# Norm pieces issued at once and Wo ahead of PV, for every chunk needed next, in a one-core transformer block

## The chip, the cores and the metric

The kernel runs on one core of a Trainium2 chip. Its engines work from queues of their own: TensorE (PE; its weight loads are shown as PEld), VectorE (DVE), ScalarE (ACT), GpSimd (POOL) and SyncE (SP, which here only issues DMA). They wait for each other by semaphores, and each runs its instructions in the order in which they were issued to it. The metric is the device time of one execution in microseconds, less is better.

## The reference

One transformer block over 2048 tokens of width 1024, batch 1, all in bfloat16: layer norm, attention with 32 query heads of 32 that share one key and one value head, a residual, a second layer norm, a gated feed-forward of width 3584, a residual.

```python
def _A_ref(x, wq, wk, wv, wo):
    q = (x @ wq).reshape(B, S, H, Dh).transpose(0, 2, 1, 3)
    k = x @ wk
    v = x @ wv
    p = softmax(einsum("bhqd,bkd->bhqk", q, k) * Dh ** -0.5)
    o = einsum("bhqk,bkd->bhqd", p, v)
    return o.transpose(0, 2, 1, 3).reshape(B, S, H * Dh) @ wo

def _B_ref(x, w_gate, w_up, w_down):
    return (sigmoid(x @ w_gate) * (x @ w_up)) @ w_down

h = x + _A_ref(layernorm(x), wq, wk, wv, wo)
h2 = h + _B_ref(layernorm(h), w_gate, w_up, w_down)
```

## The kernel before

The tokens are cut into 8 chunks of 256 (`NQC`, `QC`), each of two tiles of 128 tokens (`TPQ`). Keys, values and queries are made first. Then attention for chunk c+1 runs while the feed-forward of chunk c runs between its pieces.

**Attention** goes in 512 bursts (`NB`). A chunk has 8 groups of four heads (a group is one g = 8c + q), and a group has 8 bursts (`BPG`), each over 256 keys. `s_burst(k)` (L637) issues eight matmuls of scores into S_ps; two exponentials on ScalarE (`one_exp`, L660) turn them into P, which lies in a ring of 18 tiles, 9 bursts (`RP`); `ring_need(k)` tells how far PV must have come before burst k has a place in it. For most groups VectorE adds P over pairs of key tiles (`add_pair`: pair L694, merge L703), so that the sums of the softmax cost few matmuls (L734). `pv_group(g)` multiplies P by V (L754) in one bank of X_ps; its evacuation copies and transposes out (L772, L773), then `recip` (L778, L780) and `mult` (L784) write the group's attention output into QT. These two are put into VectorE's waiting list `lo` unless the group is the very last of chunk 0.

**Wo, residual, second norm.** When all 8 groups of a chunk have their output, four `wo_group`s (two token tiles, two halves of the width; eight matmuls of 128x512 each, L316) form the attention result. Their evacuation adds x (L844) and calls `stats2`: `bn_stats` of the half (L866), after the second half `bn_aggr` (L870), then mean, variance plus eps, and two powers on GpSimd (L331, L339, L342, L344), then `norm` on VectorE (L348) and a transposing DMA into QT (`transpose2`, L487; on SyncE's queue, for the last chunk on ScalarE's). Only for chunk 0 are the statistics issued in the evacuation itself, with the eps addition on VectorE (L873), and the norm put at the head of its list (`first`). For other chunks the pieces wait in `lo` under a chain "l0" or "l1", and are issued when `dve_fill` finds room by the planner's clock.

**Feed-forward.** Per chunk 14 gate groups and 14 up groups in turn (`half_group`, 16 matmuls of 128x256 each, L932), tanh on ScalarE (L951), the product on VectorE (L971), then four down groups (28 matmuls of 128x512 each, L996) with the evacuation L1006, which adds the residual and stores. Weights for gate and up come in halves of 512 KB through SyncE's queue into 21 places as these come free (`load_halves`). All of it stands in one list, `ffn_list`; the first gate group of a chunk may be taken only when both tiles' norms are there.

**The planner.** The order on all engines is made while the program is built, by a loop with a clock for each engine (`k_pe`, `k_dve` and others) and costs written in the code. PV, Wo, feed-forward and query groups share two X_ps banks. In each turn the loop takes the first that applies: a burst, if the ring and S_ps have room; the PV group under way; the current group if the next chunk is starved; a Wo group of chunk 0 ahead of all else (`first`); a new PV group; the current or next group of Wo, queries or feed-forward. `force` issues items of `lo` until a condition holds.

Of the kernel before, what the change touches and what calls it, by code (L numbers as in the profile page):

```python
# [84 lines left out]
def bass_sequential_preLN__grouped_kv_mqa__glu_gated_glu__prompt_kernel(  # L85
# [18 lines left out]
    NQ = D // P  # L104
    QC = 256
    NQC = S // QC
    TPQ = QC // P
# [5 lines left out]
    NB = NQC * NQ * BPG  # L113
    WSL = NQ * BPG
    RP = 18
    HR = 5
    NGU = 4
    G_SUM, NPB, NO_SUM = 3, 4, (NQ,)
    HG = 3
    WD_AT, WD_GAP, WD_LATE = 6, 6, 6  # L120
# [5 lines left out]
    with ExitStack() as es:  # L126
# [13 lines left out]
        hact_flat = sb("hact", [NFT * QC])  # L140
        gu = sb("gu", [NGU, 512], F32)
        wgu = sb("wgu", [4, DT, 256])
# [78 lines left out]
        def _(unused):  # L221
# [383 lines left out]
            def ring_need(k):  # L605

                r = ring(k)
                if r is None or r < 2 * BPG + 1:
                    return 0
                return r - 2 * BPG if r <= 2 * BPG + BPG else r - BPG  # L610
# [33 lines left out]
            pv_done = [0]  # L644
# [71 lines left out]
            def pv_group(g):  # L716
                c, q = g // NQ, g % NQ
# [51 lines left out]
                def evac(bank, tick):  # L769
                    force("a", lambda: g < 1 or g - 1 in ols_read)  # L770
                    need(dve, tick, ols_read.get(g - 1))
                    dve.tensor_copy(out=ols[:, 0:QC], in_=bank[:, 0:QC])  # L772
                    free = c_dve.inc(dve.transpose(ols[:, QC:2 * QC], bank[:, QC:2 * QC]), 0.7, 0.08)  # L773
                    t_ = [None]

                    def recip():
                        need(dve, free)
                        r_ = c_dve.inc(dve.reciprocal(l8[:], ols[:, QC:2 * QC].rearrange("p (a b) -> p a b", b=32)[:, :, 0]), 0.23)  # L778
                        need(dve, r_)
                        t_[0] = c_dve.inc(dve.transpose(ols[:, QC:2 * QC], l8[:].unsqueeze(2).to_broadcast([P, QC // 32, 32])), 0.4)  # L780

                    def mult():
                        need(dve, t_[0])
                        ot_val[(c, q)] = ols_read[g] = c_dve.inc(dve.tensor_tensor(  # L784
                            out=QT[:, q, c * QC:(c + 1) * QC], in0=ols[:, 0:QC], in1=ols[:, QC:2 * QC],
                            op=ALU.mult), 0.4)
                    if g == NQ - 1:
                        force("a", lambda: not any(x[0] == "a" for x in lo))
                        recip()
                        mult()  # L790
                    else:
                        put("a", 0.65, recip, lambda: when(free))
                        put("a", 0.4, mult, lambda: when(t_[0]))
                    return free
                return _Group(items, evac, (), "pv")


# [40 lines left out]
            def wo_group(c, tt, dc):  # L838
                t = c * TPQ + tt

                def evac(bank, tick):
                    need(dve, tick, hx_val[t])
                    hv = hx[:, t % HR, dc * 512:(dc + 1) * 512]
                    h_val[t] = c_dve.inc(dve.tensor_tensor(out=hv, in0=bank, in1=hv, op=ALU.add), 0.61, 0.08)  # L844
                    stats2(c, tt, dc)
                    if dc == DC - 1:
                        h_done.add(t)
                    return h_val[t]
                items = mm_list([(QT[:, q, c * QC + tt * P:c * QC + (tt + 1) * P], wo[:, q, dc * 512:(dc + 1) * 512])
                                 for q in range(NQ)], lambda bank: bank, 512)  # L850
                g = _Group(items, evac, [wo_val[0]] + [ot_val[(c, q)] for q in range(NQ)])
                g.first = c == 0
                return g

            ln2_pow = {}

            def stats2(c, tt, dc):
                t, first = c * TPQ + tt, c == 0
                idx = NT + t
                src = hx[:, t % HR, :]  # L860
                chain = "l%d" % (t % 2)
                h_tick = h_val[t]

                def part(cc):
                    need(dve, h_tick)
                    ins = dve.bn_stats(st[:, idx % 4, cc, :], src[:, cc * 512:(cc + 1) * 512])  # L866
                    k_dve[0] += 0.64
                    if cc == DC - 1:
                        need(dve, c_dve.inc(ins))
                        st2_val[t] = c_dve.inc(dve.bn_aggr(mv[:, idx, :], st[:, idx % 4, :, :]), 0.2)  # L870
                        if first:
                            need(dve, st2_val[t])
                            v = c_dve.inc(dve.tensor_scalar(out=vz[:, idx:idx + 1], in0=mv[:, idx:idx + 1, 1], scalar1=EPS_B,  # L873
                                                            scalar2=None, op0=ALU.add), 0.1)
                            ln2_pow[t] = ln_pow(idx, v)
                            ln_mean(idx)
                            ln2_pow[t] = (c_pool, c_pool.n)
                        else:
                            ln2_pow[t] = ln_rstd(idx, st2_val[t])

                def norm():
                    before = hn_read[t - TPQ] if c > 0 else xnT_read[NT - TPQ + tt]
                    hn_val[t] = ln_norm(src, hn[:, tt, :], idx, st2_val[t], ln2_pow[t], before)
                    transpose2(c, tt)
                if first:
                    part(dc)
                else:
                    put(chain, 0.85 if dc else 0.64, lambda: part(dc), lambda: when(h_tick))
                if dc == DC - 1:
                    put(chain, 0.5, norm, lambda: None if t not in ln2_pow or c > 0 and t - TPQ not in hn_read else  # L890
                        when(ln2_pow[t]), first)
# [52 lines left out]
            def gate_group(c, fp):  # L944
                n = c * NFP + fp
                slot = gu[:, n % NGU, :]

# [15 lines left out]
            def up_group(c, fp):  # L963
                n = c * NFP + fp
                slot = gu[:, n % NGU, :]

# [54 lines left out]
            q_list = collections.deque()  # L1021
            wo_list = collections.deque((c, tt, dc) for c in range(NQC) for tt in range(TPQ) for dc in range(DC))
            ffn_list = collections.deque()
# [7 lines left out]
            cur, pv = [None], [None]  # L1031

            def busy(g):
                return g is not None and bool(g.items)

            def wo_ready():
                if not wo_list:
                    return False
                c, tt, dc = wo_list[0]
                t = c * TPQ + tt  # L1040
                return t in hx_val and when(hx_val[t]) <= k_pe[0] and all(
                    (c, q) in ot_val and when(ot_val[(c, q)]) <= k_pe[0] for q in range(NQ))

            def wo_c():
                return wo_list[0][0] if wo_list else -1
# [82 lines left out]
            for p in range(1, BPG):  # L1128
# [11 lines left out]
                q = p + 2  # L1140
# [45 lines left out]
            while True:  # L1186
# [6 lines left out]
                kk = k[0]  # L1193
# [12 lines left out]
                if busy(pv[0]):  # L1206
                    t_ = pv[0].items[0][2]()
                    if t_ > k_pe[0] + (2.5 * T_SW if pe_mode[0] == "pv" else 0.02):
                        if not busy(cur[0]):
                            cur[0] = next_group()  # L1210
                        if busy(cur[0]):
                            run_item(cur[0])
                            continue
                        if t_ > k_pe[0] + 0.6 and can_s:
                            k_pe[0] += 0.05
                            dve_fill(k_pe[0])
                            continue
                    run_item(pv[0])
                    if not pv[0].items and pv_done[0] == NB - BPG and not pr_given[0]:
                        pr_given[0] = True  # L1220
                        for i in range(H_PR, len(halves) - 1):
                            half_free.append((i, [(c_pv, c_pv.n), (c_dve, c_dve.n)]))
                        load_halves()
                    continue
                starved = not q_list and bool(ffn_list) and ffn_list[0][0] == "g" and ffn_list[0][1] * TPQ + 1 not in h_done
                if starved and not busy(cur[0]) and wo_ready():
                    cur[0] = next_group()
                if starved and busy(cur[0]):
                    run_item(cur[0])
                    continue  # L1230
                if not busy(cur[0]) and wo_list and wo_list[0][0] == 0 and wo_ready():
                    cur[0] = next_group()
                if busy(cur[0]) and cur[0].first:
                    run_item(cur[0])
                    continue
                if pv_ready and (pe_mode[0] == "s" or not can_s) and not (busy(cur[0]) and cur[0].left() < 1.0):
# [59 lines left out]
```

## Time and profile before

| | us |
|---|---|
| median of 3 runs | 1132.54 (1132.32 to 1133.71) |
| profiled execution, its time | 1132.68 |
| profiled execution, its span | 1130.9 |
| TensorE busy | 1090.1 |
| ScalarE busy | 1006.6 |
| of it exponentials into the ring, L660 x992 | 931.8, mean 1137 ns with overlap |
| VectorE busy | 860.1 |
| pairs L694 x480 and merges L703 x360 | 324.9 and 248.0 |
| GpSimd busy | 67.4 |
| DMA, mean | 133 GB/s |

The span is what the profiler saw from the first instruction to the last; the execution's own time has 1.8 us more around it. Busy times of one engine add up to less than the span by what it idled. Matmuls overlap in the array, so a busy TensorE is not one at its peak. A window row gives, for a stretch of the span, the busy time of each engine with its instructions in brackets, the granted TensorE clock (1.00 is full), the DMA engines' mean busy share and GB/s. A row of waits gives who waited for whom: total us, times, longest. In the timeline, a bracket after an instruction is the idle time before it and what ended that.

### The profile page before, as it was taken

The page shows a single profiled execution, that of the slowest core. Times are in us where ns is not written, and L with a number is a line of the kernel's source. Part 1 is how long each engine was busy: PE and PEld are TensorE (multiplying, and loading weights), DVE is VectorE, ACT ScalarE, POOL GpSimd, SP SyncE. Part 2 cuts the span into 40 slices and gives each one's busy share as a digit, 9 for nine tenths or more (in the row PEclk, how much of TensorE's full clock was granted, in tenths as well). Part 3 has the DMA queues.
Part 4 walks back from the last instruction along what each step waited for, and adds up shares of the span by engine and source line. Part 5 has one row for each costly group of instructions (what it writes and reads, how often), then busy time and mean ns, then how long its engine had stood idle before and what let it go on. Part 6 is the DMA issues. An engine that isn't in the chain of part 4 may idle for free.

```text
span 1130.9 us, 33101 instructions
## 1 busy us (share of the span) xinstructions
PE 1090.1 (96%) x14332; PEld 660.1 (58%) x14395; DVE 860.1 (76%) x1538; ACT 1006.6 (89%) x1150; POOL 67.4 (6%) x142
## 2 busy tenths in 40 slices
PE   7999999999899999999899999999899989999998
PEld 5663447754476545764477545764377535775784
DVE  7769977778878798788887798878887788884111
ACT  6999999999999999999999999999999999990110
POOL 4410010000100000000000010000100010001000
PEclk9999999999999999999999999999999999999999
DMA  8834117860366415661266514662167522769600
GB/s 196 176 81 171 39 39 220 231 187 24 88 187 191 118 29 150 192 191 47 61 194 195 147 31 134 193 192 57 34 185 213 160 39 62 209 193 263 180 1 19
DMA packets 282065, 150.38 MB, mean 133 GB/s; under 512 B 38592, under 2 KB 276160, under 8 KB 281920
## 3 DMA queue, kind: packets, MB, share of 16 engines
q1 hardware_dynamic: 274144, 137.65, 45.2%
q0 software_dynamic: 2544, 9.44, 2.4%
q8 instruction: 113, 1.85, 0.7%
q10 hardware_dynamic: 5232, 1.18, 0.7%
q14 instruction: 32, 0.26, 0.1%
HBM read 136.18 MB, written 4.19 MB: 124 GB/s over the span
## 4 chain that ended last, share of the span: by engine, by line
PE 71%; ACT 11%; DVE 11%; issue 4%; POOL 2%; DMA 1%; DVEq 0%; ACTq 0%
PE X_ps L932 34%; PE X_ps L996 12%; PE S_ps L637 10%; ACT Pr L660 9%; PE X_ps L754 8%; PE X_ps L316 5%; DVE pairs L694 3%; DVE pairs L703 3%; PE X_ps L734 1%; DVE st L866 1%; ACT hact L660 1%; POOL sd L342 1%; DVE hx L844 1%; POOL rs L344 1%; ACT QT L660 0%
## 5 line engine op out<-in xcount | busy, mean ns | idle before, releaser
L660 ACT ACTIVATE Pr<-S_ps 128x1024 bf16<-128x1024 f32 x992 | 931.8, 1137 | 8.8 <-PE S_ps L637 8.6
L694 DVE TENSOR_TENSOR pairs<-Pr 128x1024 bf16<-128x1024 bf16 x480 | 324.9, 684 | 76.6 <-ACT Pr L660 74.4
L932 PE MATMUL X_ps<-QT,wgu 128*128 128x256 bf16 x2096 | 267.3, 274 | 0.9 <-DVE ols L773 0.7
L703 DVE TENSOR_TENSOR pairs<-pairs 128x1024 bf16<-128x1024 bf16 x360 | 248.0, 689 | 22.3 <-DVE pairs L694 0.5
L932 PEld LDWEIGHTS X_ps<-QT,wgu 128*128 128x128 bf16 x2096 | 191.7, 98 | 58.3 <-issue 34.9
L996 PE MATMUL X_ps<-zone,hact 128*128 128x512 bf16 x849 | 206.6, 380 | 11.4 <-issue 4.9
L637 PE MATMUL S_ps<-QT,kT 32*128 32x256 bf16 x4096 | 204.4, 274 | 13.5 <-ACT Pr L660 7.0
L932 PE MATMUL X_ps<-QT 128*128 128x256 bf16 x1312 | 167.0, 273 | 0.2 <-DVE ols L773 0.2
L637 PEld LDWEIGHTS S_ps<-QT,kT 32*128 32x128 bf16 x4096 | 61.2, 92 | 156.9 <-ACT Pr L660 122.9
L754 PE MATMUL X_ps<-Pr,V 128*32 128x256 bf16 x3968 | 140.7, 275 | 4.0 <-DVE ols L773 1.5
L951 ACT ACTIVATE gu<-X_ps 128x512 f32<-128x512 f32 x112 | 74.4, 665 | 76.9 <-PE X_ps L932 75.9
L996 PEld LDWEIGHTS X_ps<-zone,hact 128*128 128x128 bf16 x896 | 78.4, 97 | 110.1 <-issue 25.2
L932 PEld LDWEIGHTS X_ps<-QT 128*128 128x128 bf16 x1312 | 121.8, 98 | 31.5 <-issue 17.1
L971 DVE SCALAR_TENSOR_TENSOR hact<-gu,X_ps 128x512 bf16<-128x512 f32 x112 | 76.5, 683 | 66.8 <-PE X_ps L932 65.8
L754 PEld LDWEIGHTS X_ps<-Pr,V 128*32 128x32 bf16 x3968 | 98.2, 97 | 30.3 <-issue 17.2
L316 PE MATMUL X_ps<-zone 128*128 128x256 bf16 (+2 forms) x512 | 77.1, 290 | 3.4 <-issue 2.4
L316 PE MATMUL X_ps<-wo,QT 128*128 128x512 bf16 x240 | 59.4, 380 | 1.8 <-issue 1.6
L331 POOL CAST mean<-mv 128x1 f32<-128x1 bf16 x28 | 9.9, 353 | 789.4 <-DVE mv L870 778.5
L316 PEld LDWEIGHTS X_ps<-zone 128*128 128x128 bf16 x512 | 36.7, 97 | 33.2 <-issue 16.7
L1006 DVE SCALAR_TENSOR_TENSOR hx<-X_ps,hx 128x512 bf16<-128x512 f32 x32 | 21.9, 684 | 42.2 <-PE X_ps L996 42.1
L772 DVE COPY ols<-X_ps 128x256 f32<-128x256 f32 x64 | 27.0, 421 | 16.0 <-PE X_ps L734 13.6
L316 PEld LDWEIGHTS X_ps<-wo,QT 128*128 128x128 bf16 x256 | 22.0, 98 | 29.2 <-issue 8.6
(76 smaller groups left out, 473.5 us busy)
## 6 DMA issues: line engine op xcount, KB each, us to landing
wgu<-in_B_w_gate_dram SPq DMA_DIRECT2D x73, 512.0 KB, 4.8
wgu<-in_B_w_up_dram SPq DMA_DIRECT2D x58, 512.0 KB, 4.8
QT<-in_B_w_up_dram SPq DMA_DIRECT2D x49, 512.0 KB, 4.9
QT<-in_B_w_gate_dram SPq DMA_DIRECT2D x33, 512.0 KB, 4.8
zone<-in_B_w_down_dram POOLq DMA_DIRECT2D x14, 512.0 KB, 5.4
hx<-in_A_x_dram SPq DMA_DIRECT2D x16, 256.0 KB, 3.5
out_dram<-hx SPq DMA_DIRECT2D x32, 128.0 KB, 1.7
Pr<-in_B_w_gate_dram SPq DMA_DIRECT2D x5, 512.0 KB, 7.9
```

Source lines behind the costliest of these rows:

```text
L316: ins = pe.matmul(sel(bank), lhsT=a, rhs=b, start=(i == 0), stop=(i == last))
L637: ins = pe.matmul(S_ps[:, bank, kt * QC:(kt + 1) * QC], lhsT=kT4[DH * j:DH * (j + 1), (2 * b + kt) * P:(2 * b + kt + 1) * P], rhs=QT[DH * ...
L660: c_e.inc(act.activation(out=p_tile(k, n % 2), in_=S_ps[:, 2 * pr:2 * pr + 2, :].rearrange("p a (b q) -> p (a b) q", q=QC), func=ACTF.Exp, ...
L694: add_half[k] = slot_use[slot] = c_dve.inc(dve.tensor_tensor(out=pairs[:, slot, :].rearrange("p (j q) -> p j q", j=4), in0=p4[:, :, 0, :], ...
L703: slot_use[x] = slot_use[y] = c_dve.inc(dve.tensor_tensor(out=pairs[:, x, :], in0=pairs[:, x, :], in1=pairs[:, y, :], op=ALU.add), T_ADD, ...
L754: ins = pe.matmul(bank[DH * j:DH * (j + 1), 0:QC], lhsT=V[:, 2 * b + kt, :], rhs=rhs(j), start=first and is_sum, stop=last and not is_sum, ...
L772: dve.tensor_copy(out=ols[:, 0:QC], in_=bank[:, 0:QC])
L932: ins = pe.matmul(bank[:, j * QC:(j + 1) * QC], lhsT=halves[i][:, dt, j * P:(j + 1) * P], rhs=QT[:, dt, c * QC:(c + 1) * QC], start=(dt == ...
L951: tanh_val[n] = c_act.inc(act.activation(out=slot, in_=bank, func=ACTF.Tanh, scale=0.5), T_TANH, 0.1)
L971: hact_val[(c, 2 * fp + 1)] = gu_read[n] = c_dve.inc(dve.scalar_tensor_tensor(out=hact[:, 2 * fp:2 * fp + 2, :], in0=slot.rearrange("p (a ...
L996: ins = pe.matmul(bank, lhsT=hact[:, ft, tt * P:(tt + 1) * P], rhs=wd[:, ft, dc * 512:(dc + 1) * 512], start=(ft == 0), stop=(ft == NFT - 1))
L1006: v = c_dve.inc(dve.scalar_tensor_tensor(out=hv, in0=bank, scalar=0.5, in1=hv, op0=ALU.mult, op1=ALU.add), 0.61, 0.08)
```

## The change

A new function `urgent(c)` tells whether chunk c is needed next: no query groups are left, the list of feed-forward has at most `NEAR` = 1 down group at its head, and what follows is of chunk c. Four places use it:

- in `pv_group`, for a chunk's last group, the waiting reciprocals and products are issued and this group's own at once;
- in `stats2`, the statistics go in with the evacuation, the eps addition on VectorE, and the norm at the head of its list, as for chunk 0 before;
- `wo_group`s get the mark `first`, and the planner takes a ready Wo group as soon as no other group is under way;
- a group marked `first` is run ahead of the next PV group, but, for chunks other than 0, only while the next burst has a place for its P (`can_s0`). `wo_c()` is the chunk of the next Wo group that is left, -1 if none.

```diff
+    NEAR = 1
...
-                    if g == NQ - 1:
+                    if g == NQ - 1 or q == NQ - 1 and urgent(c):
                         force("a", lambda: not any(x[0] == "a" for x in lo))
                         recip()
                         mult()
...
-                g.first = c == 0
+                g.first = c == 0 or urgent(c)
                 return g
...
+            def urgent(c):
+
+                downs = 0
+                while downs < len(ffn_list) and ffn_list[downs][0] == "down":
+                    downs += 1
+                return not q_list and downs <= NEAR and downs < len(ffn_list) and ffn_list[downs][1] == c
+
             def stats2(c, tt, dc):
-                t, first = c * TPQ + tt, c == 0
+                t, first = c * TPQ + tt, c == 0 or urgent(c)
...
+                can_s0 = kk < NB and pv_done[0] >= ring_need(kk)
                 starved = not q_list and bool(ffn_list) and ffn_list[0][0] == "g" and ffn_list[0][1] * TPQ + 1 not in h_done
...
-                if not busy(cur[0]) and wo_list and wo_list[0][0] == 0 and wo_ready():
+                if not busy(cur[0]) and wo_list and (wo_list[0][0] == 0 or urgent(wo_list[0][0])) and wo_ready():
                     cur[0] = next_group()
-                if busy(cur[0]) and cur[0].first:
+                if busy(cur[0]) and cur[0].first and (can_s0 or wo_c() == 0):
                     run_item(cur[0])
                     continue
```

## The prediction

> **What bounds the kernel now.** I began with the page's first part, then took 28 us windows and, inside them, 4 us windows, the list of waits on TensorE, and the timeline around each chunk's turn from attention to feed-forward.
>
> ```profile
> PE 1090.1 (96%) x14332; PEld 660.1 (58%) x14395; DVE 860.1 (76%) x1538; ACT 1006.6 (89%) x1150; POOL 67.4 (6%) x142
> ```
>
> TensorE is busy for 96% and ScalarE for 89%. The kernel runs in two regimes. Up to about 1018 us ScalarE's exponentials set when a burst of scores may come; TensorE fills the time between bursts with PV, Wo and feed-forward. After the last exponential only feed-forward is left and TensorE alone sets the end. So the end moves by two things: when the bursts are through, and how much feed-forward is left then. Every TensorE gap before 1018 us is feed-forward that has to be done after it.
>
> ```profile
> 280.00:308.00 28.00, 24.59 (x330) 12.55 (x327) 25.02 (x47) 26.68 (x30) 3.93 (x8) 0.94 0.27 62
> 308.00:336.00 28.00, 27.62 (x418) 19.59 (x414) 22.51 (x40) 28.00 (x34) 0.00 (x0) 1.00 0.67 188
> 420.00:448.00 28.00, 25.59 (x354) 15.54 (x350) 24.41 (x46) 28.00 (x33) 2.70 (x6) 1.00 0.46 123
> 532.00:560.00 28.00, 24.45 (x285) 10.35 (x283) 25.08 (x47) 25.57 (x29) 4.04 (x8) 1.00 0.15 34
> 784.00:812.00 28.00, 25.68 (x304) 10.56 (x302) 24.66 (x47) 27.87 (x31) 4.03 (x8) 1.00 0.18 39
> 924.00:952.00 28.00, 24.81 (x304) 11.81 (x304) 23.92 (x43) 25.92 (x30) 0.00 (x0) 0.94 0.13 34
> ```
>
> After the window and its length come busy time of TensorE, weight loads, VectorE, ScalarE and GpSimd, then granted clock and DMA. The second row is the steady case: both engines full. The other five are the turns of chunks 1, 2, 3, 5 and 6: TensorE loses 3.41, 2.41, 3.55, 2.32 and 3.19 us, ScalarE 1.32, 0, 2.43, 0.13 and 2.08 us. Chunk 4's turn (644 to 700 us) loses 1.5 us of TensorE and nothing of ScalarE.
>
> ```profile
> PE S_ps L637 <- ACT Pr L660: 7.0, 16, 1.4
> PE X_ps L996 <- DVE hx L1006: 4.8, 2, 2.7
> PE X_ps L734 <- DVE pairs L703: 1.1, 1, 1.1
> ```
>
> Two kinds of gap. At chunks 1 and 2 TensorE has nothing between bursts: the last down group is spent and the second norm of the next chunk has not come (first row, "waiting for ScalarE"). At chunks 3 and 6 it waits for VectorE: PV holds one of the two X_ps banks, so the next down group must take the bank just filled, and its evacuation L1006 stands behind late pairs, merges and norm pieces:
>
> ```profile
> 548.82 0.68 DVE L1006 SCALAR_TENSOR_TENSOR hx<-X_ps,hx 128x512 bf16<-128x512 f32 x1
> ...
> 549.56 0.39 PE L996 MATMUL X_ps<-zone,hact 128*128 128x512 bf16 x1 [2.65 <-DVE hx L1006]
> ```
>
> **Prices.** From the chain of waits in its undisturbed last part and one unbroken run of exponentials:
>
> ```profile
> 1031.37 10.74 PE X_ps L996 x49
> ...
> 1055.06 48.91 PE X_ps L932 x448
> ```
>
> ```profile
> 261.25 37.75 ACT L660 ACTIVATE Pr<-S_ps 128x1024 bf16<-128x1024 f32 x41
> ```
>
> So 0.22 us per Wo or down matmul, 0.109 per gate or up matmul, 0.921 per exponential, 1.84 us per burst; a tanh is 0.60.
>
> **What the change does to the order.** I compared the order in which the two built programs issue, burst by burst (512 bursts, eight L637 matmuls each). It is the same through burst 128 (263.50 us). The new condition is true for the norms of chunks 1, 2 and 3 only; at chunks 4 to 7 more than one down group is still waiting at that moment. So three chunks have their norm pieces issued at once, and six eps additions (0.22 us each on GpSimd) become VectorE instructions (0.16 us each, as L873 runs at chunk 0). From burst 380 to 510 the new order is, instruction for instruction on TensorE and VectorE, the old order of bursts 252 to 382, two chunks later. That stretch can be read off the clock of before:
>
> ```profile
> 506.98 0.40 PE L637 MATMUL S_ps<-QT,kT 32*128 32x256 bf16 x8
> ...
> 762.08 0.40 PE L637 MATMUL S_ps<-QT,kT 32*128 32x256 bf16 x8
> ...
> 1013.24 0.40 PE L637 MATMUL S_ps<-QT,kT 32*128 32x256 bf16 x8
> ```
>
> These are bursts 252, 382 and 510. Chunk 5's turn becomes a copy of old chunk 3's (with its 2.65 us wait), and chunk 6's a copy of old chunk 4's, the cheap one.
>
> Step 1, bursts 128 to 380, 494.9 us before (263.50 to 758.37). At chunk 1, before has three bursts with 1.2, 0.3 and 1.2 us of TensorE work between them against 1.84 needed; in the new order the norm is issued four bursts earlier, gate matmuls stand there, and no such interval is left. At chunk 2 the old two-burst hole (0.3 and 1.6 us of work) goes too; ScalarE lost nothing there, so this returns only as feed-forward done sooner. At chunk 3 no down group changes banks under an open PV in the worst interval, so the 2.65 us wait goes. Gone from ScalarE's clock: 1.32 + 2.43 = 3.75 us. Added: 15 more gate matmuls by burst 380, one tanh more, 0.6. New waits: the statistics (0.68 each, with the 0.69 addition ahead of them) now stand before pairs, so VectorE runs behind where Wo groups and PV change banks: at chunk 1 before the last down group, at chunk 2 before the last Wo group, at chunk 4 when five late pairs are issued together. Adding VectorE's instructions of those intervals at 0.69 per pair, merge, addition or statistic and 0.55 per norm gives backlogs of 1.2 to 1.7 us at the first two, of which TensorE can hide about 0.7 in work already queued. No row shows these waits. Bounds: 0 for all, if queued bursts cover them; 13 us, if three of them cost what the chunk 3 row shows with a clock dip as below (2.65 + 1.7 each). They are nearest to small bank waits (issue-sized to 1.2 us in the list), so I take 0.5 us of ScalarE's time each, 1.5 in all. Sum -3.75 + 0.6 + 1.5 = -1.65; burst 380 at 756.7.
>
> Step 2, bursts 380 to 510: 762.08 - 506.98 = 255.1. Burst 510 at 1011.8.
>
> Step 3, the rest: 1130.9 - 1013.24 = 117.7 us before. At burst 510 before still has 62 gate and up matmuls of chunk 6 to do, the new order 5; the 112 down matmuls, Wo, chunk 7 and PV are the same. 57 x 0.109 = 6.2, leaving 111.5. The end: 1123.3.
>
> The profiled execution took 1132.68 with a span of 1130.9, 1.8 more; the median of before is 1132.54, so the two stand for each other. Forecast 1123.3 + 1.8 = **1125.1 us**, 7.4 less.
>
> **What lies beside other work, and loses cover.** Chunk 7's norm: its last transpose, issued at 1034.9, landed within 7.8 us, 12.4 before the first gate matmul at 1055.06. The new tail has one down group (6.0) and one up group (1.75) less behind Wo: 4.6 us of cover are left, so I cost it at nothing; without cover it would be paid in full beyond 4.6. SyncE's queue: the transposes of chunks 1 to 3 (1.24 us each to issue) pass at most one store or x load each; weight loads behind them are idle in the down phase (DMA 0.02 to 0.35). The 21 halves for chunk 7 were issued by 1044 us, 11 before use, and in the new order the last is needed 21 x 1.74 us after the first: hidden. GpSimd has nothing else to do there; its shorter chain (1.6 us from aggregate to norm at chunk 0, 2.2 at chunk 1) helps VectorE. PV of group 15 has its reciprocal and product forced at once, 1.1 us on VectorE, in an interval followed by two empty ones: nothing.
>
> **Clock.** Windows of 4 us:
>
> ```profile
> 296.00:300.00 4.00, 2.63 (x57) 0.85 0.71 135
> 300.00:304.00 4.00, 4.00 (x37) 0.72 0.01 2
> ...
> 548.00:552.00 4.00, 2.18 (x57) 1.00 0.66 164
> ```
>
> After chunk 1's hole the granted clock is 0.85, then 0.72: (0.15 + 0.28) x 4 = 1.7 us of TensorE, and again at 924 to 932. After chunk 3's single gap of 2.65 it stays 1.00. [...]
>
> **Rivals.**
> 1. No new waits. TensorE's own account speaks for it: the five rows and chunk 4's turn add up to 16.4 us idle and 3.4 of lost clock; the copies keep 3.55 and 1.5, and four clean turns at about 1.3 would make 5.2, a fall of 9.5, so 1132.7 - 9.5 = 1123.2; the sum above without its 1.5 gives 1123.6. Against it, VectorE's backlogs above. Time about 1123.4.
> 2. The holes come back as bank waits: new waits at chunks 1 to 4 eat what chunks 1 and 3 gave ScalarE (1.5 + 3.75). For it: the chunk 3 row, where a planned switch met a late VectorE. 1125.1 + 3.75 = 1128.9.
> 3. Slower: VectorE becomes the bound at the turns. Its busy 25 of 28 us there leaves little room, and norm work now goes first; pairs come late, L1006 and L844 behind them, and TensorE waits 2.65 plus a 1.7 dip at each of chunks 1, 2 and 4. 1125.1 - 1.5 + 13.05 = 1136.7. It decides from about 9 us of new waits on, two such holes. Against it: the two empty intervals that follow each burst of VectorE work in the new order.
> That the change does nothing is ruled out: the issue orders differ from burst 129 on.
>
> **How the numbers follow.** Forecast 0.60 (1124 to 1127.5), rival 1 0.15, rival 2 0.15, rival 3 0.10. A change within 0.2% (2.3 us) can't be told from none here, so faster means below 1130.3. Forecast, rival 1 and 0.11 of rival 2 lie there: 0.86; the rest of rival 2 and a little of rival 3 are the same, 0.05; slower 0.09. The range 1121.8 to 1130.8 takes in rivals 1 and 2 and a part of the unknown waits, and leaves the far ones out.
>
> **What would show it.** Right: at chunk 1's and 2's turns no row with less than 26.5 of 28 us TensorE and no clock below 1.00 near 300 us; chunk 5's turn with one wait of about 2.65 on L1006; chunk 6's without; burst 510 near 1011.8 and the run of chunk 7's gate and up matmuls starting near 1047.5 and unbroken. Wrong: waits over 1.5 us on L844 or L1006 at chunks 1 to 4, late exponentials there, or a gap before chunk 7's first gate matmul. The forecast fails above all if burst 380 comes later than 758.4.

## The result and the profile after

| | before | after |
|---|---|---|
| median, us | 1133.12 (1132.32 to 1134.8, 4 runs) | 1125.34 (1122.56 to 1125.86, 4 runs) |
| profiled execution, its time and span, us | 1132.68, 1130.9 | 1125.86, 1124.1 |

The ratio of the two is 0.9927 (0.9911 to 0.9944): the changed kernel is faster by 0.7%, at 1125.3 where 1125.1 was forecast. The first part of the page of the changed kernel, its engines:

```profile
PE 1090.0 (97%) x14333; PEld 658.7 (59%) x14395; DVE 861.9 (77%) x1544; ACT 1006.7 (90%) x1150; POOL 64.0 (6%) x136
```

TensorE and ScalarE are as busy as before to 0.1 us. VectorE has six instructions more and GpSimd six fewer, the eps additions of three chunks. The span fell by 6.8 us, and TensorE's idle time, span less busy time, from 40.8 to 34.1: the gain is filled gaps.

The same five windows of 28 us as before, of the changed kernel, the turns of chunks 1, 2, 3, 5 and 6:

```profile
280.00:308.00 28.00, 26.17 (x370) 14.55 (x361) 26.18 (x50) 27.48 (x32) 2.87 (x6) 1.00 0.35 90
420.00:448.00 28.00, 27.84 (x383) 18.39 (x381) 25.64 (x48) 28.00 (x33) 0.00 (x0) 1.00 0.56 158
532.00:560.00 28.00, 27.38 (x352) 13.82 (x345) 26.12 (x50) 28.00 (x33) 2.78 (x6) 1.00 0.32 77
784.00:812.00 28.00, 24.38 (x251) 10.25 (x254) 23.95 (x44) 24.32 (x27) 4.04 (x8) 0.94 0.16 34
924.00:952.00 28.00, 27.54 (x356) 15.44 (x358) 25.60 (x47) 28.00 (x33) 2.12 (x4) 1.00 0.34 93
```

Three of the five rows are nearly full, with ScalarE at 28.00 as in the steady row of before; chunk 1's has gained, to 26.17 us of TensorE. Chunk 5's turn alone is worse than before: 24.38 us of TensorE against 25.68, 24.32 of ScalarE against 27.87, and a clock of 0.94. In the timeline that turn looks like this:

```profile
794.86 1.43 DVE L704 TENSOR_TENSOR pairs<-pairs 128x1024 bf16<-128x1024 bf16 x2
...
796.73 0.55 DVE L349 TENSOR_SCALAR hn<-hx,mean,rs 128x1024 bf16<-128x1024 bf16 x1 [0.44 <-POOL rs L345]
797.20 0.69 DVE L695 TENSOR_TENSOR pairs<-Pr 128x1024 bf16<-128x1024 bf16 x1
...
797.99 0.69 DVE L704 TENSOR_TENSOR pairs<-pairs 128x1024 bf16<-128x1024 bf16 x1
...
798.60 0.68 DVE L1014 SCALAR_TENSOR_TENSOR hx<-X_ps,hx 128x512 bf16<-128x512 f32 x1
...
799.34 0.39 PE L1004 MATMUL X_ps<-zone,hact 128*128 128x512 bf16 x1 [2.67 <-DVE hx L1014]
...
800.09 1.94 ACT L661 ACTIVATE Pr<-S_ps 128x1024 bf16<-128x1024 f32 x2 [2.44 <-PE S_ps L638]
```

It reads as chunk 3's turn did before. A down group is done, its evacuation L1014 (L1006 before) stands on VectorE behind two merges, a norm that itself waited 0.44 us for GpSimd, a pair and a merge; TensorE waits 2.67 us for the bank, the scores behind it come late, and ScalarE loses 2.44. Windows of 4 us at that place show what the old turn did not have:

```profile
794.00:798.00 4.00, 2.51 (x38) 0.97 (x30) 3.35 (x8) 3.65 (x4) 2.20 (x4) 1.00 0.00 0
798.00:802.00 4.00, 2.44 (x49) 1.47 (x50) 3.90 (x7) 1.91 (x2) 0.00 (x0) 0.82 0.70 164
802.00:806.00 4.00, 3.75 (x27) 1.31 (x28) 3.26 (x8) 2.76 (x4) 0.00 (x0) 0.75 0.02 4
```

The clock falls to 0.82, then 0.75: (0.18 + 0.25) x 4 = 1.7 us of TensorE.

The starts of bursts 252, 380 and 510 in the timeline of the changed kernel, and the end of its chain of waits:

```profile
506.83 0.40 PE L638 MATMUL S_ps<-QT,kT 32*128 32x256 bf16 x8
...
756.66 0.40 PE L638 MATMUL S_ps<-QT,kT 32*128 32x256 bf16 x8
...
1013.39 0.40 PE L638 MATMUL S_ps<-QT,kT 32*128 32x256 bf16 x8
```

```profile
1043.13 5.13 PE X_ps L1004 x23
1048.26 48.91 PE X_ps L940 x448
1097.22 10.74 PE X_ps L1004 x49
```

So the bursts are through at the same time as before (1013.39 against 1013.24), and the whole gain lies behind them: the gate run of chunk 7 starts at 1048.26 instead of 1055.06, 6.8 earlier, and is as long and as unbroken as it was. The feed-forward that the fuller turns took up isn't left for the end: 5 gate and up matmuls of chunk 6 stand behind burst 510, where 62 stood before.

### The profile page after: what moved, and what is told of

Its sections match the earlier page's. It is cut to its first block, busy times and chain, and to the rows that moved or that the text cites. A ratio compares the mean times of both kernels' runs of the same rounds, so it can differ in the third digit from the quotient of the medians.

```text
span 1124.1 us, 33106 instructions
## 1 busy us (share of the span) xinstructions
PE 1090.0 (97%) x14333; PEld 658.7 (59%) x14395; DVE 861.9 (77%) x1544; ACT 1006.7 (90%) x1150; POOL 64.0 (6%) x136
## 3 DMA queue, kind: packets, MB, share of 16 engines
q10 hardware_dynamic: 5232, 1.18, 0.6%
## 4 chain that ended last, share of the span: by engine, by line
PE 78%; ACT 10%; DVE 6%; issue 3%; POOL 1%; DMA 1%; DVEq 0%; ACTq 0%
PE X_ps L940 35%; PE X_ps L1004 15%; PE S_ps L638 12%; PE X_ps L755 9%; ACT Pr L661 8%; PE X_ps L317 6%; DVE pairs L704 2%; DVE pairs L695 1%; PE X_ps L735 1%; ACT hact L661 1%; POOL sd L343 1%; DVE st L874 1%; DMA zone<-zone 0%; ACT QT L661 0%; DVE hx L845 0%
## 5 line engine op out<-in xcount | busy, mean ns | idle before, releaser
L940 PE MATMUL X_ps<-QT 128*128 128x256 bf16 x1328 | 170.0, 273 | 0.0
L1014 DVE SCALAR_TENSOR_TENSOR hx<-X_ps,hx 128x512 bf16<-128x512 f32 x32 | 21.9, 685 | 36.3 <-PE X_ps L1004 36.1
L343 POOL TENSOR_TENSOR sd<-vz,powers 128x1 bf16<-128x1 bf16 x32 | 21.7, 678 | 340.7 <-DVE vz L881 329.3
L773 DVE COPY ols<-X_ps 128x256 f32<-128x256 f32 x64 | 27.0, 422 | 12.1 <-PE X_ps L735 9.8
```

What stands on the lines that cost most here:

```text
L343: t_ = c_pool.inc(pool.tensor_tensor(out=sd[:, i:i + 1], in0=vz[:, i:i + 1], in1=half[:, 0:1], op=ALU.pow), 0.6)
L940: ins = pe.matmul(bank[:, j * QC:(j + 1) * QC], lhsT=halves[i][:, dt, j * P:(j + 1) * P], rhs=QT[:, dt, c * QC:(c + 1) * QC], start=(dt == ...
```

## The experiments

Two questions lead them. Which part of the change gives the gain, and can chunk 5's copied turn be mended? Each time below is a median with its range, and each ratio is to the kernel before on the same chip.

**1. Chunk 5's turn: the norm behind the pairs.** `force` issues a ready norm piece at the head of the list ahead of the pairs that it is called for. In chunk 5's turn it no longer may:

```diff
-                    if lo[0][0][0] == "l":
+                    if lo[0][0][0] == "l" and not (chain == "p" and 395 < k[0] < 415):
```

> TensorE's order is that of the changed kernel throughout. Only in bursts 395 to 415, at chunk 5's turn, the waiting pieces of the second norm are no longer pulled ahead of the pairs, so VectorE reaches the evacuation of the down group without two statistics and one norm before it. Theory (the 2.67 us wait of TensorE there is VectorE's lateness, and norm pieces are 1.4 us of it): the wait falls to about 1.2 us or less and, with a shorter gap, the clock stays at 1.00 (the after profile had 0.82 and 0.75 there, 1.7 us). Time 1122 to 1124. Rival (the wait is set by the bank and the pairs alone): the wait stays over 2.3 us and the time is 1125.3 within 0.7.

Measured: 1121.41 us (1120.86 to 1122.04), ratio 0.9898 (0.9883 to 0.9913). The timeline of this kernel at the place, and its window of the turn:

```profile
795.10 0.69 DVE L1014 SCALAR_TENSOR_TENSOR hx<-X_ps,hx 128x512 bf16<-128x512 f32 x1
...
795.85 0.39 PE L1004 MATMUL X_ps<-zone,hact 128*128 128x512 bf16 x1 [0.93 <-DVE hx L1014]
...
796.30 0.69 DVE L874 BATCH_NORM_STATS2 st<-hx 128x6 f32<-128x512 bf16 x1
```

```profile
784.00:812.00 28.00, 27.07 (x352) 12.61 (x352) 25.02 (x47) 27.30 (x31) 3.13 (x6) 1.00 0.26 67
```

The statistics now stand behind the evacuation. The wait is 0.93 instead of 2.67 us, the clock stays at 1.00, and ScalarE gets 27.30 of 28 us instead of 24.32. TensorE's order is the same as in the changed kernel. From burst 400 to 414 the changed kernel takes 4.6 us longer than before, this one 1.4: the difference of 3.2 us is wait and clock dip, and it arrives at the end almost whole. The theory that VectorE's order in this one turn costs the change some 3 us is borne out, and the time is a little below what it gave.

**2. The forced reciprocal undone.** The first of the four places goes back:

```diff
-                    if g == NQ - 1 or q == NQ - 1 and urgent(c):
+                    if g == NQ - 1:
```

> The changed kernel without the forced reciprocal and product of a chunk's last group; from burst 133 on TensorE and VectorE have the same order as the changed kernel. Theory (that part does nothing, since Wo cannot start before down(0,1,0) ends): 1125.3 within 1. Rival (Wo comes sooner because of it): slower by 2 us or more. It is also a second look at chunk 5's wait of 2.67 us: the order is the same, so whether the clock dips there again tells if the dip belongs to the order.

Measured: 1124.05 us (1123.15 to 1126.01), ratio 0.9924 (0.9909 to 0.9938): as the changed kernel. This part gives nothing and costs nothing. Chunk 5's turn has its wait (2.6) and its dip (0.88, then 0.69) here too.

**3. Chunk 1 alone.**

```diff
-                return not q_list and downs <= NEAR and downs < len(ffn_list) and ffn_list[downs][1] == c
+                return c in (1,) and not q_list and downs <= NEAR and downs < len(ffn_list) and ffn_list[downs][1] == c
```

> The condition holds for chunk 1 alone. From burst 316 the order is that of before from burst 252, one chunk later. Theory (the gain is what the turns lose, and one turn changed moves all later ones to other old patterns): chunk 1's 1.32 us of ScalarE are gained, old chunk 3's wait moves to chunk 4, old chunk 4's cheap turn to chunk 5, old chunk 6's wait (2.08) is gone, 25 gate and up matmuls fewer (2.7 us) are left at burst 510: 1133.1 - 1.3 - 2.1 - 2.7 + 0.5 = 1127.5, up to 1.7 more if the clock dips at chunk 4. Rival (each of the three chunks gives a third of the gain on its own): 1130.5.

Measured: 1128.05 us (1127.24 to 1130.79), ratio 0.9962 (0.9951 to 0.9973). Windows of chunks 4's and 5's turns:

```profile
672.00:700.00 28.00, 26.51 (x342) 15.36 (x342) 22.82 (x41) 24.58 (x29) 0.00 (x0) 0.94 0.39 114
784.00:812.00 28.00, 27.97 (x338) 11.62 (x330) 25.96 (x49) 28.00 (x32) 3.96 (x8) 1.00 0.19 35
```

The time lies within what the theory gave. The expensive turn has moved to chunk 4 (ScalarE 24.58, clock 0.94), with a wait of 2.65 us on L1014, and chunk 5's is full. So each chunk that is treated moves the pattern of the turns on by some, and the wait isn't bound to chunk 5: it sits where that order falls.

**4 and 5. The two halves by themselves.** Wo ahead of PV, with the norm's pieces as before:

```diff
-                    if g == NQ - 1 or q == NQ - 1 and urgent(c):
+                    if g == NQ - 1:
...
-                t, first = c * TPQ + tt, c == 0 or urgent(c)
+                t, first = c * TPQ + tt, c == 0
```

> Wo groups of the chunk needed next go ahead of PV, statistics and norm stay in the waiting list as before. From burst 252 on the order is that of before. Theory (the norm pieces standing in the list make the holes, Wo's place does not): the holes at chunks 1 and 2 stay, by the work between bursts 3.0 and 4.4 us against 4.4 and 2.4 before, time 1133 within 1.5. Rival (Wo ahead of PV carries the gain): 1129 or less.

Measured: 1133.43 us (1131.54 to 1137.43), ratio 1.001 (0.9999 to 1.0021), no gain. Its windows of chunks 1's and 2's turns:

```profile
280.00:308.00 28.00, 25.43 (x326) 13.71 (x326) 25.13 (x47) 26.69 (x31) 4.13 (x8) 0.94 0.32 81
420.00:448.00 28.00, 24.79 (x338) 15.47 (x340) 23.95 (x44) 26.95 (x32) 2.12 (x4) 0.94 0.44 119
```

The holes stay, since gate matmuls cannot start without the norm. The other half, the norm's pieces at once with Wo in its old place:

```diff
-                    if g == NQ - 1 or q == NQ - 1 and urgent(c):
+                    if g == NQ - 1:
...
-                g.first = c == 0 or urgent(c)
+                g.first = c == 0
...
-                if not busy(cur[0]) and wo_list and (wo_list[0][0] == 0 or urgent(wo_list[0][0])) and wo_ready():
+                if not busy(cur[0]) and wo_list and wo_list[0][0] == 0 and wo_ready():
...
-                if busy(cur[0]) and cur[0].first and (can_s0 or wo_c() == 0):
+                if busy(cur[0]) and cur[0].first:
```

> The second norm's pieces of chunks 1 to 3 go in at once; Wo's place, the reciprocal and the ring condition stay as before. From burst 340 the order is that of before from burst 276, one chunk later. Theory (the norm pieces carry most of the gain, Wo's place adds a part): chunk 1's 1.3 us, old chunk 3's 2.4 and old chunk 6's 2.1 of ScalarE are gone, 2.7 us less feed-forward is left at burst 510, 0.5 for a tanh, 1 to 2 us of new waits at chunk 3 where VectorE's backlog is 4.5 us by its instructions: 1126, between 1124.5 and 1127.5. Rival (norm and Wo must move together): 1130 or more.

Measured: 1132.38 us (1131.79 to 1135.18), ratio 0.9998 (0.9988 to 1.0008). A miss: no gain here either, where I had expected most of it. Its timeline at chunk 3's turn:

```profile
552.67 1.42 DVE L704 TENSOR_TENSOR pairs<-pairs 128x1024 bf16<-128x1024 bf16 x2
554.00 0.42 DVE L773 COPY ols<-X_ps 128x256 f32<-128x256 f32 x1
554.34 0.44 DVE L774 STREAM_TRANSPOSE ols<-X_ps 128x256 f32<-128x256 f32 x1
...
555.03 0.37 PE L940 MATMUL X_ps<-QT,wgu 128*128 128x256 bf16 x1 [3.91 <-DVE ols L774]
...
555.99 1.94 ACT L661 ACTIVATE Pr<-S_ps 128x1024 bf16<-128x1024 f32 x2 [3.92 <-PE S_ps L638]
```

From 547.28 to 554.00 VectorE runs ten pairs and merges without a break, and PV's copy out and the down group's evacuation stand behind them; in the changed kernel the evacuation runs at 549.06, between pairs. With Wo late the early norm makes a wait of 3.91 us out of the 2.65 that it was to remove, and ScalarE loses as much. Bursts 276 to 284 alone take 5.8 us more than before, and a second such turn follows at chunk 4 (3.0, bursts 332 to 340); behind each the clock dips (0.94 in both windows of 28 us). What other turns gain goes into these. Apart from the reciprocal, which experiment 2 shows to be worth nothing, this kernel differs from the changed one only in Wo's place. In these orders the two halves work together only. Whether the norm's half would gain by itself with VectorE's queue reordered at those two turns, as experiment 1 does for one, was not tried.

**6. One reordering in the kernel before.** The exception of experiment 1, in the old kernel and at its chunk 3, `267 < k[0] < 287` in place of the range there:

```diff
-                    if lo[0][0][0] == "l":
+                    if lo[0][0][0] == "l" and not (chain == "p" and (267 < k[0] < 287)):
```

> The kernel before, but in bursts 267 to 287 the waiting norm pieces are not pulled ahead of the pairs; TensorE's order is that of before throughout. Theory (chunk 3's 2.65 us wait is VectorE's lateness there): the wait falls to about 0.9 us as in e1, ScalarE's 2.43 us to about 0.7, time 1130.9 against 1132.6. Rival (such a gap is made up later, since ScalarE is not always the bound): no change, 1132.6 within 0.7.

Measured: 1129.18 us (1129.03 to 1130.96), ratio 0.9967 (0.9955 to 0.9979). Its windows of chunks 3's and 6's turns:

```profile
532.00:560.00 28.00, 26.18 (x307) 11.56 (x312) 25.56 (x48) 27.29 (x30) 4.13 (x8) 1.00 0.16 37
924.00:952.00 28.00, 26.84 (x388) 13.93 (x392) 24.66 (x44) 27.36 (x32) 0.00 (x0) 1.00 0.20 57
```

The bursts gain 1.7 us between 268 and 276, as expected. Another 1.5 comes between 414 and 470, with no edit there: chunk 6's turn has its wait still (2.1 us on L1006), but the clock stays at 1.00 where before it fell to 0.94; why, no run shows. By the median the time is below what was expected.

**7, 8 and 10. How many chunks.** `urgent` for chunks 1 to 4, whatever stands in the list, with an exception at chunk 6's turn:

```diff
-    NEAR = 1
+    NEAR = 4
...
-                    if lo[0][0][0] == "l":
+                    if lo[0][0][0] == "l" and not (chain == "p" and (459 < k[0] < 479)):
...
-                return not q_list and downs <= NEAR and downs < len(ffn_list) and ffn_list[downs][1] == c
+                return c in (1,2,3,4) and not q_list and downs <= NEAR and downs < len(ffn_list) and ffn_list[downs][1] == c
```

> The condition holds for chunks 1 to 4 whatever number of down groups is still waiting, and in bursts 459 to 479 (chunk 6's turn, where the old chunk 3 pattern comes to stand) norm pieces are not pulled ahead of pairs. Theory: 2.7 us less feed-forward is left at burst 510 than in the changed kernel; against e1 (1121.4) that is -2.7 + 0.5 for a tanh + about 1 of new waits at chunk 4: 1120.2, between 1119 and 1122. Rival (VectorE's backlog of 4.4 us by its instructions at chunks 3 and 4 costs TensorE waits of 2.5 us each): 1124 or more.

Measured: 1122.38 us (1122.22 to 1123.42), ratio 0.9905 (0.989 to 0.992), just outside the 1119 to 1122 that was expected and some 2 us short of its middle. A new wait in its timeline at chunk 4 is longer than the 1 us that was allowed for:

```profile
658.62 0.39 PE L1004 MATMUL X_ps<-zone,hact 128*128 128x512 bf16 x1 [2.30 <-DVE hx L845]
```

Every chunk (`NEAR = 4` and nothing else):

```diff
-    NEAR = 1
+    NEAR = 4
```

> The condition holds at every chunk from 1 to 7, with up to four down groups waiting. The old chunk 3 pattern comes at no turn; 0.8 us less feed-forward is left at burst 510 than in the changed kernel. Theory (what counts is that no turn has a hole or a late evacuation under an open PV): 1125.3 - 2.4 - 0.8 + 0.5 to 1.5 of new waits = 1122.6 to 1123.6, or 1.7 less if the clock dips nowhere. Rival (norm pieces ahead of pairs at every chunk make VectorE the bound): 1127 or more.

Measured: 1123.65 us (1122.4 to 1125.87), ratio 0.9916 (0.99 to 0.9932), not to be told from the changed kernel; the 2.3 us wait of chunk 4 is here too. Treating a chunk that has down groups left brings in a wait of the kind that it was to avoid. And fewer chunks, 1 and 2:

```diff
-                return not q_list and downs <= NEAR and downs < len(ffn_list) and ffn_list[downs][1] == c
+                return c in (1, 2) and not q_list and downs <= NEAR and downs < len(ffn_list) and ffn_list[downs][1] == c
```

> The condition holds for chunks 1 and 2 alone; through burst 263 the order is that of the changed kernel. Theory (a turn's loss depends on where its evacuations fall, not on how many norms went early): up to burst 252 within 0.5 us of the changed kernel; after it holes of about 2 us in TensorE's work at chunks 3, 4 and 5 and 3.6 us more feed-forward left at burst 510: 1127 to 1129. Rival (two of three chunks give two thirds of the gain): 1128. The two agree on the time; the windows at chunks 4 and 5 tell them apart: theory 26 of 28 us or less of TensorE there, rival the changed kernel's 27.2 at chunk 4 and 24.4 at chunk 5.

Measured: 1126.43 us (1125.55 to 1127.25), ratio 0.9942 (0.9927 to 0.9957), a little below both expectations. Windows of chunks 3's, 4's and 5's turns:

```profile
532.00:560.00 28.00, 24.67 (x311) 11.74 (x312) 24.97 (x47) 27.11 (x31) 4.91 (x8) 1.00 0.24 60
672.00:700.00 28.00, 27.84 (x398) 17.20 (x398) 24.21 (x43) 28.00 (x33) 0.00 (x0) 1.00 0.47 133
784.00:812.00 28.00, 24.73 (x326) 10.35 (x329) 24.48 (x45) 27.25 (x31) 4.90 (x8) 1.00 0.15 34
```

TensorE loses 3.3 us at chunks 3 and 5, and the clock stays at 1.00 there. Chunks 4 and 5 were to tell the two accounts apart, and they do not: chunk 5 has the theory's hole, though the rival's row was close to it, and chunk 4 has 27.84 of 28 us, where the theory said 26 or less. So the theory missed chunk 4. Treating chunk 3 too is worth 2.3 us, by the changed kernel's 1124.08 on the same chip (experiment 11).

**9. Without the place for P.** Wo of an urgent chunk goes ahead of PV whether or not the next burst has a place:

```diff
-                if busy(cur[0]) and cur[0].first and (can_s0 or wo_c() == 0):
+                if busy(cur[0]) and cur[0].first:
```

> The changed kernel without the condition that the next burst has a place for its P: Wo groups of the chunk needed next always go ahead of PV. Then the condition holds at all chunks and every turn has the same order. By the work between bursts some 10 us more ScalarE time passes up to burst 510 (about 1.7 at each of six turns, exponentials that wait for a place in the ring), and some 10 us less feed-forward is left there. Theory (the end is the sum of the two): 1123 to 1126, ScalarE at each turn about 26.3 of 28 us. Rival (the exponentials lost can't be given back): 1130 or more.

Measured: 1127.35 us (1126.49 to 1128.36), ratio 0.9948 (0.9934 to 0.9962), later than expected by 1.4 at the least. The end of its chain of waits, in which the row of DMA is chunk 7's norm on its way through the transpose into QT:

```profile
1023.49 3.83 PE X_ps L1004 x17
1027.32 3.47 PE X_ps L317 x16
1034.67 7.13 DMA QT<-hn
1041.80 5.16 issue
1046.95 50.84 PE X_ps L940 x448
```

TensorE has nothing for 6.7 us ahead of the gate run. Behind Wo it has a single down group (28 matmuls, 1034.28 to 1040.27); the second transpose is issued at 1038.4 only and transposes land 7.1 to 8.5 us after their issue, at 1045.5 at the earliest, against a gate run that starts at 1046.95. In the changed kernel the transposes are through the queue by 1036.6 and down matmuls fill the time to 1048.3. So much more feed-forward was done early that what should cover the last norm was gone. From burst 128 to 510 it takes 3.9 us more than the changed kernel (753.4 against 749.4), where some 10 were expected. From burst 510 (1016.2) to the gate run pass 30.8 us, 24.1 without the gap, against 34.9 in the changed kernel. A version with this order and a cover for the norm was not tried.

**11 and 12. The changed kernel and experiment 1's again**, with no further edit, side by side on one chip.

> The changed kernel beside e12 on one chip. Theory: 1124.7 within 1, ratio 0.992 to 0.994.

Measured: 1124.08 us (1123.85 to 1124.95), ratio 0.9921 (0.9909 to 0.9934).

> The kernel of e1 beside e11 on one chip. Theory: 1121.5 within 1, about 3 us under e11, with the wait at chunk 5 near 0.9 us and no clock below 1.00 there. Rival (e1 was a lucky set of runs): within 1.5 us of e11.

Measured: 1121.26 us (1120.85 to 1122.04), ratio 0.9895 (0.9881 to 0.9908). Chunk 5's turn, first of the changed kernel and then of the other:

```profile
784.00:812.00 28.00, 24.61 (x282) 11.02 (x289) 23.99 (x43) 24.35 (x28) 3.04 (x6) 0.94 0.17 39
```

```profile
784.00:812.00 28.00, 26.34 (x338) 12.30 (x341) 25.38 (x47) 27.30 (x32) 4.13 (x8) 1.00 0.22 54
```

The ranges do not touch: 2.8 us between the medians, most of them in this turn. The version with pairs first at chunk 5 beats both kernels.

## Why the prediction was right

The mechanism held: fuller turns at chunks 1 to 3, a copied turn at chunk 5, and the gain in what is left behind burst 510. That the time came out 0.2 us from the forecast is partly luck. The start and the three steps were off by +0.45, -0.5, +1.6 and -0.8 us, which add up to 0.8 only; the median lies 0.5 under the profiled execution; and the same kernel's median was 1124.08 in experiment 11.

**The copy.** That bursts 380 to 510 repeat old bursts 252 to 382 was the strongest step, and the copied turn came with its wait: 2.67 us on L1014 where 2.65 had been read. Reading a future stretch off the clock of an old one, when the order is the same, held to 0.6% here.

**Step 1** (burst 380 at 756.7) came out at 756.66. By parts, from the starts of bursts 128, 252, 276 and 380 in both traces: chunk 1's turn gave 0.60 us, chunk 3's 2.74, and from 276 to 380 the new order lost 1.18, the tanh and the new waits; together 2.16 where 1.65 was forecast. Burst 128, ahead of any difference, came 0.45 later in this execution, which hid the surplus. The 1.5 us for new waits, taken near the low end of bounds 0 to 13, were about right: what the list of waits shows of them is 1.0 us on L845 at chunk 1. Experiment 5 shows that the upper part of the bounds was real. Had Wo stayed behind, one such wait would have been 3.91 us.

**Step 2** (255.1 from burst 380 to 510) was mis-sized: it took 256.7. The copied wait had the old length, but a clock dip of 1.7 us behind it, which the old turn did not have, and that is the whole difference. The prediction read the clock of the copied turn off the old one and so put a dip there at nothing. Experiments 2 and 11 have the dip at the same place, so three of three profiles with this turn, and experiment 3 has it at chunk 4, while the old turn at chunk 3 ran at 1.00 before and in experiment 4. The order, copied instruction for instruction, brought the wait with it, but not the clock: behind the wait it is 0.50 for 3.41 us in the copy and 1.00 in the old turn, with 1.24 us of TensorE work in the 3.41 us ahead in both (the last section has the windows). What sets the two apart, no run shows.

**Step 3** (111.5 left after burst 510) was mis-sized by 0.8 the other way: 110.7. Everything from the gate run on is as before to the hundredth (1124.1 - 1048.26 and 1130.9 - 1055.06 are both 75.84), so the 57 matmuls and what lies around them were worth 6.95 us instead of 6.2. Of the rest, 0.24 us is a wait for PV's transpose (L773) that the kernel before has at 1020.32 and the new tail has not; what made the remainder was not followed. The two errors left 0.8 us in the span, 1124.1 against 1123.3.

**The cover** of chunk 7's norm held: its second transpose was out of the queue at 1036.6, landings there took 8.2 us in the median of the two, and the gate run began at 1048.26 without a gap, so some 3.5 to 4.9 us of cover were left where 4.6 were named. Experiment 9 shows the price when it is gone, 6.7 us.

**What was to be seen.** Chunk 1's row stayed under its mark (26.17 where 26.5 was named), with the clock at 1.00 as named; chunk 2's (27.84), chunk 5's wait, chunk 6's clean turn and the gate run's start (1048.26 for 1047.5) came as written. Burst 510 came 1.6 us later than named (1013.39 for 1011.8), by the dip of step 2. The waits over 1.5 us that would have shown it wrong did not come: the longest on L845 or L1014 at chunks 1 to 4 is 1.0 us.

**What the prediction had in the wrong place** is the source of the gain. It credited the norm's pieces and treated Wo's place as part of the same order. Experiments 4 and 5 show that each half by itself is worth nothing (1133.4 and 1132.4): the norm pieces fill TensorE's holes, and Wo ahead of PV is what keeps the price of that from being paid in a bank wait at chunk 3. The sum came close because it was made from the order of the whole.

**Rivals.** No new waits (1123.4) was near, and the time alone can't rule it out: the changed kernel's executions took 1122.56 to 1125.86 us. The trace does, by the wait of 1.00 us at chunk 1 and the 1.18 lost from burst 276 to 380; what put the time above 1123.4 is the dip of 1.7. Holes coming back as bank waits is what half of the change does (experiment 5), and what treating more chunks does at chunk 4 (experiments 7 and 8). VectorE as the bound did not come: it is busy for 24 to 26 of 28 us at the turns, as before.

## What to carry to other kernels

When an engine runs its queue in order, look at what stands ahead of the instruction that frees a bank: moving statistics and a norm behind one evacuation gave 2.8 us with TensorE's order unchanged (the shorter wait, and the clock dip that it spared), about a third of what the whole change gave. Work that is done early saves time only while something is left to cover the last latency, here a transpose of some 8 us; count that cover before moving more. And judge the parts of a change that belong together by the order that they make together, since each alone may show nothing.

## What the runs showed of the hardware

The same gap, and the same order, came with a clock dip and without. The gap of TensorE of 2.1 us at chunk 6 had a clock of 0.94 in the window of 28 us in the kernel before and 1.00 in experiment 6; the gap of 2.6 to 2.7 with one order of matmuls had no dip at chunk 3, one in three of three at chunk 5 and one at chunk 4 in experiment 3.

Between 36 and 1100 us the profile of the kernel before has two dips, from 298.81 and from 926.87, and that of the changed kernel has one, from 800.58. Each is a stretch of 3.41 us at a clock of 0.50. The one of the changed kernel, with the stretch of the same length ahead of it:

```profile
797.17:800.58 3.41, 1.24 (x33) 0.80 (x37) 3.31 (x7) 0.97 (x2) 0.00 (x0) 1.00 0.57 99
800.58:804.00 3.42, 2.95 (x39) 1.25 (x29) 3.25 (x8) 2.55 (x4) 0.00 (x0) 0.50 0.28 98
```

In the kernel before, at the same distance from the same wait at chunk 3, TensorE is busy for 1.24 us of 547.39 to 550.80 as well, and the clock is 1.00 there and from 550.80 to 554.21. So the length of the gap and the TensorE work around it do not tell the two turns apart. What does, these runs do not show, and none was made to test it.

Each of these dips costs about 1.7 us (half of 3.41), and the gap ahead of the one at chunk 5 another 2.67. After the long gap of experiment 9 (6.7 us) the first 16 gate matmuls took 3.57 us, in the changed kernel 1.91; the clock from 1040 to 1060 was 0.83 in experiment 9.

The start varies: burst 128, up to which all these kernels issue alike, came between 262.04 and 263.95 us. Profiles of single executions are therefore best compared by the time between two bursts, not by the time of one. The mean clock varies too, and with it the time: at 0.997 executions of the kernel before took 1131.45 and 1131.53 us, at 0.992 between 1132.65 and 1135.27.
